# Two small loads issued by ScalarE's queue in place of SyncE's, and seven rounds of warming products in place of nine

## The chip, the cores and the metric

The kernel runs on one core of a Trainium2 chip. The metric is the device time of one execution in microseconds, as the median of several runs; lower is better. Engines are named as in the profile: PE is TensorE, DVE is VectorE, ACT is ScalarE, POOL is GpSimd, SP is SyncE. SPq and ACTq are the queues of SP and of ScalarE from which transfers are issued.

## The reference

Attention over 4 batches, 8 heads, 768 positions and 64 values a head, in which each row sees a few global positions and a local band before it, with a bias that grows with the distance; its output goes through a feed-forward layer of 512 to 2048 to 512 with a leaky activation whose slopes `alpha` are an input.

```python
scores = scale * np.matmul(q, k.transpose(0, 1, 3, 2))
keep = is_global | is_local            # from n_global = 8 and n_local = 96
scores = np.where(keep, scores - slopes * dist, -1e9)
a = softmax(scores)
x = np.matmul(a, v)                    # laid out as (3072, 512)
h = x @ w_in
g = np.maximum(h, 0.0) + alpha * np.minimum(h, 0.0)
return (g @ w_out).astype(np.float32)
```

`n_global` and `n_local` are two integers of 64 bits; they and `alpha` (2048 numbers) are the two small loads of the change. All else of the input is large.

## The kernel before

The 3072 tokens are cut into twelve units of 256. For each unit the kernel computes attention for eight heads, two at a time, then transposes the result and multiplies it with the two weight matrices, in 16 slices of 128 columns. The weights are loaded as float32 and split into two float16 parts each. Units 0 and 1 are prepared in a plain way in float32, so that work can begin before the weights are there.

The order on every engine is written out. `fast` (line 379) enters each step into a `Plan` (line 150) with a key, an engine and a cost; `Plan.order` (line 189) plays these through with costs and lags (180 after POOL, 220 after ACT, 150 after DVE, 1100 after SP, and for SP 525 an issue and 1125 before a transfer moves), and `Plan.emit` (line 293) writes the instructions in the order of the planned starts. Each engine then works through its own instructions strictly in that order.

The steps that matter here:

- `body` (line 1499) begins with the identity, the tile `ones` (line 1505), and the load of the integers into `ni` (line 1508). VectorE casts these to `nf` (line 1517).
- `warm` (line 1326) enters `WARM` products of `ones` with itself as the first step of TensorE, at the planned cost `WARM * 200`. Nothing reads their result. Each float32 product appears as two records in the trace.
- `build_bias` (line 449): POOL writes the column numbers, ScalarE makes `part` (line 484) and then the constants `ends` (line 486), VectorE builds the masks `D` from `nf` and `part` (lines 471 to 481), and eight products, `D` times a slope each, go to ScalarE or VectorE (lines 400 and 401).
- `load_first` (line 663): for unit 0, SP loads queries and keys of two heads at a time (line 677), then the values (lines 672 and 683). Behind the last of the value loads, for head 6, the same step calls `load_alpha`, defined in line 1541. `ak` (line 687) on VectorE is alpha's first reader.
- `score_pair` (line 824) enters the first scores (line 725), preceded at some places by `keep_busy` products (line 705). VectorE adds the bias and takes the smallest of the negated scores of each row (line 865), ScalarE takes the exponentials (line 875 for unit 0, line 879 for unit 1), TensorE transposes (line 908), ScalarE or VectorE copies (lines 914 and 915), TensorE multiplies with the values (line 954).
- `v_load` (line 508) and `v_sums` (line 514): the sums over the values of batch 0, from the first loads, from `firstv` and from `rawv` (line 529), from which a scale for float16 is made through a product on TensorE (`vrow`, line 555). The transposes `xp` (line 1122) and their copies `xt` (line 400) need that scale.

```python
def warm(key):
    x = buf("av", "warm", [P, 512])
    def products():
        for n in range(WARM):
            nc.tensor.matmul(x.t[:, :P], lhsT=cn["ones"], rhs=cn["ones"], start=True, stop=True)
    op("PE", key, WARM * 200, products, w=[x])
...
def values():
    nc.sync.dma_start(out=x.t[:, nk:n], in_=a["first0"][h // 2, :, nk:])
    if h == 6:
        cn["load_alpha"]()
```

Of the kernel before, what the change touches and what calls it, by code (L numbers as in the profile page):

```python
# [17 lines left out]
I32 = mybir.dt.int32  # L18
# [323 lines left out]
WLEAD = 12  # L342
VS = 6
VL = 5
WARM = 9
XPOOL, SPOOL = 0, (0, 1, 2, 3, 4, 5, 6, 7)
V0LATER, ENDS = 1, 20
F1, F1S, W0, W0S = -65, 0.5, -59, 2
# [30 lines left out]
def fast(tc, cn, a, finish):  # L379
# [3 lines left out]
    with ctx:  # L383
# [8 lines left out]
        def op(eng, key, cost, fn, r=(), w=()):  # L392
            plan.op(key, r, w, (eng, cost, fn))
# [932 lines left out]
        def warm(key):  # L1326
# [3 lines left out]
# [6 lines that stand above are left out]
# [163 lines left out]
def body(tc, a):  # L1499
    nc = tc.nc  # L1500
    with tc.tile_pool(name="const", bufs=1) as cp:
        ident = cp.tile([P, P], F32, name="ident")
        make_identity(nc, ident)
        ones = cp.tile([P, P], F32, name="ones")
        nc.vector.memset(ones, 1.0)
        alpha = cp.tile([P, NF], F32, name="alpha")
        ni = cp.tile([P, 4], I32, name="ni")
        nc.sync.dma_start(out=ni, in_=a["n"].bitcast(I32))
        nf = cp.tile([P, 4], F32, name="nf")
        n2 = cp.tile([P, 2], F32, name="n2")  # L1510
        tt = cp.tile([P, 2], F32, name="tt")
        mx = cp.tile([P, 8], F32, name="mx")
        ck = cp.tile([P, 12], F32, name="ck")
        flag = cp.tile([P, 1], I32, name="flag")
        v = nc.vector

        v.tensor_copy(out=nf, in_=ni)
        low, high = (nf.rearrange("p (n t) -> p n t", t=2)[:, :, t] for t in range(2))

        def check(line):  # L1520
            v.scalar_tensor_tensor(out=tt[:, 0:2], in0=low, scalar=0.0, in1=high, op0=ALU.is_lt, op1=ALU.add)
            v.scalar_tensor_tensor(out=n2, in0=tt[:, 0:2], scalar=4294967296.0, in1=low, op0=ALU.mult, op1=ALU.add)
            v.tensor_copy(out=mx[0:1, 4:8], in_=line)
            for j, (x, lo, hi) in enumerate((
                (n2[0:1, 0:1], 0.0, float(GL)), (n2[0:1, 1:2], 1.0, float(LOC + 1)),
                (mx[0:1, 4:5], -3.0e38, 1.0), (mx[0:1, 5:6], *RI), (mx[0:1, 6:7], *RO), (mx[0:1, 7:8], -1.0, -1.0),
            )):
                v.tensor_scalar(out=ck[0:1, 2 * j : 2 * j + 1], in0=x, scalar1=lo, scalar2=None, op0=ALU.is_ge)
                v.tensor_scalar(out=ck[0:1, 2 * j + 1 : 2 * j + 2], in0=x, scalar1=hi, scalar2=None, op0=ALU.is_le)
            v.tensor_reduce(out=tt[0:1, 0:1], in_=ck[0:1, :], axis=AX.X, op=ALU.min)  # L1530
            v.tensor_scalar(out=flag[0:1, :], in0=tt[0:1, 0:1], scalar1=1.0, scalar2=None, op0=ALU.is_lt)

        path = []

        def choose():
            path.append(nc.values_load(flag[0:1, 0:1], min_val=0, max_val=1))
            tc.mark_branch_hint_location("general", hint=path[0], engines=[
                mybir.EngineType.PE, mybir.EngineType.DVE, mybir.EngineType.Activation, mybir.EngineType.SP])

        cn = dict(ident=ident, ones=ones, alpha=alpha, ngf=n2[:, 0:1], nlf=n2[:, 1:2], check=check, choose=choose, maxima=mx, nf=nf,  # L1540
                  load_alpha=lambda: nc.sync.dma_start(out=alpha, in_=a["alpha"]))
        def finish(last):
            with tc.If(path[0] > 0, label="general") as chosen:
                general(tc, cn, a)
            with chosen.Else():
                last()

        fast(tc, cn, a, finish)
# [14 lines left out]
```

## Time and profile before

| | |
|---|---|
| median of 3 runs | 582.86 us |
| lowest, highest | 582.19, 583.93 us |
| profiled execution | 582.48 us |
| its span, first to last instruction | 580.7 us |
| TensorE busy | 567.9 us (98%) |
| VectorE busy | 487.7 us (84%) |
| ScalarE busy | 427.4 us (74%) |
| GpSimd busy | 81.0 us (14%) |
| mean granted clock of TensorE | 0.997 of full speed |

The page gives shares over the whole span. The change touches the first ten microseconds, so the tables by stretch and the timeline of the start are what to read; there each row is a group of instructions of one line with its start, its length, and in brackets how long its engine sat idle before it and what ended that.

### The profile page before, as it was taken

The page shows a single profiled execution, that of the slowest core. Times are in us where ns is not written, and L with a number is a line of the kernel's source. Part 1 is how long each engine was busy: PE and PEld are TensorE (multiplying, and loading weights), DVE is VectorE, ACT ScalarE, POOL GpSimd, SP SyncE. Part 2 cuts the span into 40 slices and gives each one's busy share as a digit, 9 for nine tenths or more (in the row PEclk, how much of TensorE's full clock was granted, in tenths as well). Part 3 has the DMA queues.
Part 4 walks back from the last instruction along what each step waited for, and adds up shares of the span by engine and source line. Part 5 has one row for each costly group of instructions (what it writes and reads, how often), then busy time and mean ns, then how long its engine had stood idle before and what let it go on. Part 6 is the DMA issues. An engine that isn't in the chain of part 4 may idle for free. (4 is left out here: it accounts for less than half of the span.)

```text
span 580.7 us, 20234 instructions
## 1 busy us (share of the span) xinstructions
PE 567.9 (98%) x8133; PEld 405.9 (70%) x8133; DVE 487.7 (84%) x1438; ACT 427.4 (74%) x1129; POOL 81.0 (14%) x194
## 2 busy tenths in 40 slices
PE   8789999999999999999999999999999999999997
PEld 7666666676666676777776777777767777767785
DVE  7899999998898898889889789789889878675443
ACT  8799999988789878776777778677578668553322
POOL 2002334223333232000001000001000000000000
PEclk9899999999999999999999999999999999999999
DMA  8997597338575279329887854528863872210001
GB/s 278 408 375 223 168 218 196 68 71 184 112 118 126 49 174 272 90 65 241 197 175 149 185 156 115 142 53 225 203 176 82 175 175 36 69 26 1 37 5 41
DMA packets 93830, 85.04 MB, mean 146 GB/s; under 512 B 71968, under 2 KB 72736, under 8 KB 93728
## 3 DMA queue, kind: packets, MB, share of 16 engines
q1 hardware_dynamic: 93584, 83.54, 57.5%
q8 instruction: 65, 1.06, 0.8%
q14 instruction: 37, 0.30, 0.2%
q10 hardware_dynamic: 144, 0.13, 0.1%
HBM read 56.65 MB, written 6.29 MB: 108 GB/s over the span
## 5 line engine op out<-in xcount | busy, mean ns | idle before, releaser
L1296 PE MATMUL o<-whl,gh 128*128 128x512 f16 (+1 forms) x800 | 230.3, 371 | 0.0
L1296 PE MATMUL o<-whl,gl 128*128 128x512 f16 (+1 forms) x400 | 148.2, 371 | 0.5 <-POOL gl L426 0.5
L1296 PEld LDWEIGHTS <-gh 128*128 128x128 f16 x800 | 71.6, 98 | 50.9
L1234 PEld LDWEIGHTS <-sw 128*128 128x128 f16 x1536 | 92.3, 98 | 14.3 <-issue 0.9
L1146 PE MATMUL h<-xt,whl 128*128 128x256 f16 x768 | 91.7, 273 | 0.9 <-DVE xt L427 0.7
L1146 PEld LDWEIGHTS <-whl 128*128 128x128 f16 x768 | 74.3, 98 | 18.6 <-issue 1.2
L879 ACT ACTIVATE pr<-pr,sm 128x192 f32<-128x192 f32 (+1 forms) x176 | 77.2, 441 | 4.0 <-DVE sm L865 3.8
L1234 PEld LDWEIGHTS <-whl 128*128 128x128 f16 x1152 | 69.6, 98 | 12.9 <-issue 0.2
L1296 PEld LDWEIGHTS <-gl 128*128 128x128 f16 x400 | 39.1, 98 | 44.8 <-POOL gl L426 1.0
L426 POOL TENSOR_TENSOR gl<-g,gh 128x256 f16<-128x256 f32 x58 | 48.8, 843 | 104.9 <-ACT gh L1161 69.0
L400 ACT ACTIVATE gh<-ga 128x512 f16<-128x512 f32 x32 | 20.2, 630 | 58.6 <-DVE ga L1273 58.6
L865 DVE CUSTOM_DVE_ANT_0 pr<-sp,D 128x192 f32<-128x192 f32 (+1 forms) x192 | 56.6, 339 | 3.7 <-PE sp L725 3.1
L1234 PE MATMUL ha<-xt,sw 128*128 128x128 f16 x768 | 53.3, 219 | 0.3 <-ACT p L1241 0.3
L1234 PE MATMUL hc<-xt,sw 128*128 128x128 f16 x768 | 53.3, 219 | 0.2 <-DVE ga L1245 0.2
L1234 PE MATMUL ha<-xt,whl 128*128 128x128 f16 x768 | 53.5, 219 | 0.0
L1004 ACT ACTIVATE ps<-pr,sm 128x192 f16<-128x192 f32 (+1 forms) x120 | 45.1, 439 | 9.7 <-DVE sm L896 4.9
L1008 DVE SCALAR_TENSOR_TENSOR ps<-pr,sm,ps 128x192 f16<-128x192 f32 (+1 forms) x128 | 47.9, 416 | 2.3 <-ACT ps L1004 2.0
L893 POOL TENSOR_SCALAR sm<-sm 128x4 f32<-128x4 f32 (+1 forms) x42 | 10.7, 254 | 245.3 <-ACT pr L879 244.7
L427 DVE SCALAR_TENSOR_TENSOR gl<-ga,gh 128x512 f16<-128x512 f32 x32 | 22.0, 689 | 13.9 <-ACT gh L400 13.8
L879 ACT ACTIVATION_READ_ACCUMULATOR pr<-pr,sm 128x1 f32 x176 | 33.5, 190 | 0.0
L427 DVE SCALAR_TENSOR_TENSOR x<-raw,x 128x672 f16<-128x672 f32 (+1 forms) x40 | 33.3, 835 | 0.1
L400 ACT ACTIVATE x<-raw 128x672 f16<-128x672 f32 (+1 forms) x33 | 24.1, 731 | 12.6 <-PE sp L725 12.4
(172 smaller groups left out, 964.9 us busy)
## 6 DMA issues: line engine op xcount, KB each, us to landing
w<-in_w_dram SPq DMA_DIRECT2D x32, 512.0 KB, 7.4
again<-in_w_dram SPq DMA_DIRECT2D x32, 512.0 KB, 5.1
raw<-in_qk_dram SPq DMA_DIRECT2D x28, 336.0 KB, 3.4
out_dram<-os SPq DMA_DIRECT2D x23, 256.0 KB, 2.9
rawv<-in_own_dram SPq DMA_DIRECT2D x10, 512.0 KB, 4.7
raw<-in_qk_dram SPq DMA_DIRECT2D x12, 272.0 KB, 3.0
gp<-v SPq DMA_DIRECT2D x48, 64.0 KB, 2.0
first<-in_qk_dram SPq DMA_DIRECT2D x4, 336.0 KB, 5.4
```

Source lines behind the costliest of these rows:

```text
L400: lambda: nc.scalar.mul(out=out(), in_=src(), mul=by.t if tile_ else by)),
L426: return e.tensor_tensor(out=out(), in0=src(), in1=hi(), op=ALU.subtract)
L427: return e.scalar_tensor_tensor(out=out(), in0=src(), scalar=val(), in1=hi(), op0=ALU.mult, op1=ALU.subtract)
L865: op("DVE", key, c_dve(n) + 10, lambda t=t, m=m, n=n, dc=dc: v.tensor_tensor_reduce(out=taken(t, m), in0=three(sp.t[:, 192 * t : 192 * t + ...
L879: op("ACT", key + 1, c_act(n, ptr=1) + 93, lambda t=t, m=m: nc.scalar.activation(out=taken(t, m), in_=taken(t, m), func=AF.Exp, bias=sm.t[ ...
L893: op("POOL", key + soon, c_pool(2 * G), lambda: nc.gpsimd.tensor_scalar(out=sm.t[:, 4 * G : 6 * G], in0=sm.t[:, 2 * G : 4 * G], scalar1=1e ...
L1004: ("ACT", c_act(n, ptr=1), lambda hi=hi, src=src, by=by: nc.scalar.mul(out=hi(), in_=src(), mul=by())),
L1008: ("DVE", Two(c_dve(n, False, 1)), lambda hi=hi, lo=lo, src=src, by=by: v.scalar_tensor_tensor(out=lo(), in0=src(), scalar=by(), in1=hi(), ...
L1146: nc.tensor.matmul(hp.t, lhsT=w.t[:, wi, wc], rhs=x.t[:, NC * xi + c, :], start=n == 0, stop=n == 3 * NC - 1)
L1234: nc.tensor.matmul(out, lhsT=weight(name, f, wi, c), rhs=x.t[:, 8 * piece + m * xi + 2 * j + c, :], start=start and p == n == 0, stop=n == ...
L1296: nc.tensor.matmul(o.t[:, cols], lhsT=g_()[:, tok], rhs=w.t[:, wi, 512 + cols.start : 512 + cols.stop], start=f == 0 and n == 0, stop=f == ...
```

## The change

The load of the integers (`ni`) and that of the slopes (`alpha`) are issued by ScalarE's queue and no longer by SyncE's. Their places in the code are the same: `ni` at the head of `body`, `alpha` behind the last of unit 0's value loads. The warming step has seven products and not nine, and its planned cost is 1400 and not 1800.

```diff
-WARM = 9
+WARM = 7
...
-        nc.sync.dma_start(out=ni, in_=a["n"].bitcast(I32))
+        nc.scalar.dma_start(out=ni, in_=a["n"].bitcast(I32))
...
-                  load_alpha=lambda: nc.sync.dma_start(out=alpha, in_=a["alpha"]))
+                  load_alpha=lambda: nc.scalar.dma_start(out=alpha, in_=a["alpha"]))
```

## Rows read from the trace of the kernel before

**Rows 1.** The page's engine shares: busy us, share of the span, instructions.
```profile
PE 567.9 (98%) x8133; PEld 405.9 (70%) x8133; DVE 487.7 (84%) x1438; ACT 427.4 (74%) x1129; POOL 81.0 (14%) x194
```
**Rows 2.** Stretches: us, busy PE, PEld, DVE, ACT, POOL; granted clock; DMA share; GB/s.
```profile
3.00:4.00 1.00, 1.00 (x7) 1.00 (x7) 0.95 (x3) 0.92 (x1) 0.00 (x0) 1.00 1.01 370
...
23.00:24.00 1.00, 0.58 (x4) 0.41 (x3) 0.93 (x8) 1.00 (x3) 0.00 (x0) 0.50 1.00 406
...
30.00:32.00 2.00, 2.00 (x68) 1.69 (x69) 2.00 (x8) 2.00 (x10) 0.10 (x1) 1.00 1.01 391
...
300.00:400.00 100.00, 100.00 (x1611) 71.80 (x1610) 86.82 (x263) 74.03 (x209) 6.16 (x22) 1.00 0.57 139
```
**Rows 3.** Timeline 0 to 9 us: start, length, engine, line, tiles; idle before and releaser.
```profile
0.73 1.28 ACT L484 ACT_TABLE_LOAD   x1 [0.73 <-PEq L1553]
0.73 0.39 SPq L1508 DMA_DIRECT2D ni<-in_n_dram  x1
...
1.05 4.21 PE L1332 MATMUL warm<-ones 128*128 128x128 f32 x18 [1.05 <-DVE ones L1505]
1.18 1.84 SPq L677 DMA_DIRECT2D first<-in_first_dram  x4
...
2.13 0.42 ACT L484 ACTIVATE part<-rel 128x256 f32<-128x256 f32 x1
...
2.40 0.35 DVE L1517 CAST nf<-ni 128x4 f32<-128x4 int32 x1 [1.41 <-DMA ni<-in_n_dram]
...
2.86 0.83 DVE L474 SCALAR_TENSOR_TENSOR D<-rel,nf,part 64x192 f32<-64x192 f32 x2
...
4.90 1.91 ACT L400 ACTIVATE D<-D 128x320 bf16<-128x320 f32 x5 [0.98 <-DVE D L481]
...
5.19 1.62 PE L725 MATMUL sp<-first 64*64 64x128 f32 x32
...
6.42 0.43 SPq L1541 DMA_DIRECT2D alpha<-in_alpha_dram  x1
...
6.77 2.24 ACT L875 ACTIVATE pr<-pr,sm 128x128 f32<-128x128 f32 x6
...
7.39 1.13 PE L705 MATMUL sp<-ident 128*128 128x128 f32 x8 [0.58 <-DVE sm L865]
```
**Rows 4.** Timeline 10 to 22 us, one engine at a time: alpha's reader, and four waits.
```profile
10.68 0.17 DVE L687 TENSOR_SCALAR ak<-alpha 128x16 f32<-128x16 f32 x1
...
16.50 0.69 DVE L529 TENSOR_REDUCE vm<-firstv 128x1 f32<-128x512 f32 x1 [1.04 <-DMA firstv<-in_first1v_dram]
...
17.49 0.46 ACT L879 ACTIVATE pr<-pr,sm 128x192 f32<-128x192 f32 x1 [1.47 <-DVE sm L865]
...
18.60 0.69 DVE L529 TENSOR_REDUCE vm<-rawv 128x1 f32<-128x512 f32 x1 [0.28 <-DMA rawv<-in_own_dram]
...
21.35 0.35 PE L555 MATMUL vrow<-vdg,ones 128*128 128x128 f32 x1 [2.41 <-DVE vdg L549]
```
**Rows 5.** DMA issues: queue, count, KB each, us to landing; last, ScalarE's issue (timeline).
```profile
first<-in_first_dram SPq DMA_DIRECT2D x1, 272.0 KB, 2.9
ni<-in_n_dram SPq DMA_DIRECT2D x1, 2.0 KB, 1.6
alpha<-in_alpha_dram SPq DMA_DIRECT2D x1, 8.0 KB, 4.2
rawv<-in_own_dram SPq DMA_DIRECT2D x1, 512.0 KB, 8.1
out_dram<-os ACTq DMA_DIRECT2D x1, 128.0 KB, 2.0
...
577.21 0.38 ACTq L1313 DMA_DIRECT2D out_dram<-os  x1
```
**Rows 6.** Timeline of ScalarE at 25 us: start, length, line, tiles; idle before and releaser.
```profile
25.39 0.69 ACT L400 ACTIVATE xt<-xp,vs 128x512 f16<-128x512 f32 x1 [0.86 <-PE xp L1122]
```

## The prediction

> **What bounds the kernel now.** I read the page's engine shares first, then a table of stretches, then the timeline of the first 24 us, and last the DMA landings. TensorE is busy 98% of the span [rows 1]. The table says where that is not so: from 300 to 400 us TensorE is busy 100.00 of 100.00 us, while from 30 to 32 us VectorE and ScalarE are both at 2.00 of 2.00 [rows 2]. So the body is bound by TensorE, and the first 50 us by VectorE and ScalarE, which run without a stop from about 20 us on. What happens earlier therefore counts only by how much it moves the time at which these two get going. No instruction of the body is changed, so what is gained or lost at the start arrives unchanged at the end, or is swallowed on the way.
>
> Before 20 us there are three chains.
> (a) The transfers. The share of the DMA engines is 1.01 from 3 to 4 us and stays near or above 1 up to 40 us [rows 2]. VectorE, at 16.50, has sat 1.04 us idle for `firstv`, and at 18.60 another 0.28 us for `rawv`; ScalarE sat 1.47 us before 17.49 [rows 4]. `rawv` leads to the row of maxima, for which TensorE sits idle 2.41 us up to 21.35 [rows 4]. So at 16 to 19 us the transfers end last, and every computing engine has spare time.
> (b) The bias chain on VectorE and ScalarE: `ni` lands, is cast at 2.40, the masks end in five products `D` on ScalarE from 4.90, and the exponentials follow from 6.77 without a gap [rows 3].
> (c) TensorE: 18 records of warming from 1.05 for 4.21 us, then the first scores at 5.19 [rows 3]. Their data, issued at 1.18, landed 2.9 us later, at 4.1 [rows 3, 5]: the scores waited for the warming, not for the data.
>
> **SP loses the load of `ni`.** SP issues `ni` at 0.73 (0.39 us) and starts on the four first loads at 1.18 [rows 3]. With `ni` gone, these start at 0.73: 0.45 us earlier, and with them the whole queue of transfers, which is issued in order and from 3 us on limited by the engines. Bytes stay the same, so I take the full 0.45 us for `firstv` and `rawv`. The lower bound is 0, if the two issues at 0.73 hold each other up, which no row shows. The upper bound adds alpha's 0.43 us of issue [rows 3], 0.88 in all; I take nothing of that, as at a DMA share of 1.0 an issue that comes sooner only queues longer: `rawv` took 8.1 us from issue to landing against 2.9 for the first load [rows 5].
>
> The Trainium skill (DMA: Bandwidth & Descriptors, "Rules for kernel authors") says that spreading loads over several issuing engines gives no bandwidth, since all use the same 16 DMA engines, and saves the sequencer's issue time only. The DMA share of 1.01 in [rows 2] agrees; by that rule the gain is the 0.45 us and not more.
>
> **ScalarE gets `ni`.** Its first work is the table load at 0.73 (1.28 us) [rows 3]. If the issue stands ahead of that, as its place in the code has it, it costs ScalarE about the 0.38 us of its one issue in this trace [rows 5]. `ni` then lands between 2.33 (1.6 us after issue, as on SP) and 2.73 (2.0 us, as ScalarE's store) [rows 5], 0 to 0.4 us later than now. The table load ends 0.38 later, so `part` at 2.13 also comes about 0.38 later; VectorE's first use of it, at 2.86, starts some 0.3 us after `part` is ready at 2.55 [rows 3], so 0.1 us of delay is left. `ends`, next on ScalarE, moves into the 0.98 us of idle time before 4.90 [rows 3]. The bias chain is 0.1 to 0.4 us late; I take 0.1, since the first row for `ni` itself is the 1.6.
>
> **ScalarE gets `alpha`.** Its issue sits in the emission after the last of the value loads. The planner gives SP 525 ns an issue, so the tenth load stands at 9 x 525 = 4725; the products `D` start there at 1500 + 180 + 325 + 220 + 1590 + 150 = 3965 (GpSimd's columns, `part`, the masks, and the lag after each) and take 381 each. The issue thus stands before or behind the third of the five `D` on ScalarE. Queued behind it are the remaining `D` and six exponentials, and for these wait the first transposes on TensorE and VectorE's next scores. Cost: 0.43 us (its issue on SP [rows 3]; 0.38 by ScalarE's store [rows 5]), and nothing if it should fall into the idle 0.98 us before 4.90 [rows 3]. I take 0.43. The reader of alpha, `ak` at 10.68 [rows 4], does not wait: issued near 5.7 and 4.2 us on the way [rows 5], alpha lands by 9.9.
>
> **Two rounds of warming less.** Four of the 18 records go, at 4.21/18 = 0.23 us about 0.9 us [rows 3]. The first scores can start near 4.3 and not 5.19; their data, at 4.1 - 0.45 = 3.65, are there. But the exponentials stand behind five `D` on ScalarE, which start when the bias chain allows: ScalarE runs from 4.90 into the exponentials at 6.77 without a break [rows 3]. The 0.9 us becomes idle time of TensorE and VectorE; I cost it at 0. Its bound on the good side is also small, since at 16.5 us the transfers come last anyway. The planner's cost of the step falls from 1800 to 1400, but it lets the scores start only after their load, at 1125 + 1148 + 1100 = 3373, so the order written out for the engines should be the same.
>
> **The sum.** Chain (b) is late by 0.1 + 0.43 = 0.53 us (bounds 0.0 and 0.83). Its cover: VectorE would have been at the `rawv` reduction 1.04 + 0.28 = 1.32 us before 18.60, at 17.28. Late by 0.53 it is there at 17.81, and `rawv` now allows 18.60 - 0.45 = 18.15. The gain stays whole up to a delay of 1.32 - 0.45 = 0.87 us, and the change turns into a loss beyond 1.32 us. So -0.45 us from 18.6 us on, carried to the end. The profiled execution is 582.48 us (span 580.7 and 1.78 around it): 582.03. The median shown is 582.86, 0.38 higher; the middle of the four executions known (582.19, 582.48, 582.86, 583.93) is 582.67, and 582.67 - 0.45 = **582.2 us**. What a measurement of this kernel can tell from no change is about 0.3%, 1.75 us; the forecast lies well inside.
>
> **Rivals.**
> *Clock, slower.* The 18 warming products took 4.21 us where eight of the same shape and type at 7.39 took 1.13 [rows 3]: 0.23 against 0.14 us each. So the warming ran at the lower level (1.2 GHz) and the later ones at 2.4 GHz, although the table prints no lower clock there. Before the rise TensorE had been in work without a break since 1.05. With the change there is 0.9 us less of that, and a longer pause before 7.39. The Trainium skill (TensorE: Matmul & The Clock Gate, "Part 1: The HAM clock gate") has the slow level as the default, which activity releases; by that rule less early work can put the rise off. Price: after the idle stretch before 21.35 the clock fell to 0.50 at 23 to 24 us [rows 2], and ScalarE waited 0.86 us for transposes made in it [rows 6]. Three such stretches, from 6 to 16 us, would be 2.6 us, and up to 3.9 if VectorE's waits add half. With chain (b)'s 0.53 that is 3.1 to 4.4 against a cover of 1.32: +1.8 to +3.1, **584.5 to 585.8**. It decides from two such stretches on (1.7 + 0.53 = 2.25, +0.9, 583.6); one is covered (0.86 + 0.53 = 1.39, +0.1). Against it: the scores follow the warming directly and the fills at 7.39 were made to go on.
> *ScalarE late.* If the table load is put ahead of the issue of `ni`, `ni` goes out at 0.73 + 1.28 = 2.01 and the bias chain is 1.28 late, with alpha 1.71: 0.39 beyond the cover, **583.1**. For it: the table load is ScalarE's first record. Against: it carries line 484, behind the place of the load.
> *No gain.* The issues at 0.73 hold each other up, or some later wait that both kernels share swallows 0.45 us: **582.7**.
> *More gain.* SP, freed of alpha too, runs 0.88 us ahead, and chain (b) is less late than 0.44: **581.8**.
>
> **How the numbers follow.** Forecast 0.45; no gain 0.18; ScalarE late 0.17; more gain 0.11; clock 0.09. The range reaches from the lowest execution with the larger gain, 582.19 - 0.88 = 581.3, rounded out to 581.1, to the lower end of the clock case, 584.5, rounded to 584.4, which also covers the highest execution, 583.93, with 0.4 on top. Over 0.3% slower means above 584.6: most of the clock case, 0.08. Over 0.3% faster means under 581.1: nothing above gives that; I leave 0.05 for a clock that falls for a shorter time around 23 us.
>
> **What the profile after would show.** The step on SP is right if the first load is issued at 0.7 to 0.8 and the wait for `rawv` ends at about 18.1. The step on ScalarE is right if the cast of `ni` starts between 2.4 and 2.8, `D` at about 5.0, and the exponentials at about 7.3. The warming is right if its record counts 14, the scores start near 4.3, and VectorE's idle time before 9.4 grows. The prediction is wrong if the cast comes at 3.5 or later (table load first), if the granted clock is low for long stretches between 6 and 20 us, if VectorE reaches the `rawv` reduction after its data, or if the time is kept at 19 us and lost later.

## The result, and the profile after

The changed kernel takes 587.31 us in the median of 8 runs (584.41 to 590.35), the kernel before 582.70 in the same comparison. The ratio is 1.0075, with a 95% interval of 1.0056 to 1.0094: slower by about 4.4 us. Two further comparisons of the same two kernels, below, gave 1.0052 [1.0032, 1.0073] and 1.0055 [1.0034, 1.0075], so 3 to 4.4 us is the size. The forecast was 582.2, with a range up to 584.4; the sign and the size were wrong. The ratios are those of the comparisons and not the quotients of the medians, which here would be 1.0079.

The profiled execution is the slowest of the eight: 590.35 us, span 588.6. Its timeline of the first 12 us, to be read against [rows 3] (start, length, engine, line, operation and tiles; in brackets the idle time before and what ended it):

```profile
0.73 0.41 ACTq L1508 DMA_DIRECT2D ni<-in_n_dram  x1
0.73 1.82 SPq L677 DMA_DIRECT2D first<-in_first_dram  x4
1.05 3.36 PE L1332 MATMUL warm<-ones 128*128 128x128 f32 x14 [1.05 <-DVE ones L1505]
1.17 1.28 ACT L484 ACT_TABLE_LOAD   x1 [1.17 <-PEq L1553]
...
2.79 1.47 ACT L486 ACTIVATE ends<-ones 128x1536 f16<-128x1536 f32 x1
...
3.77 0.17 DVE L1517 CAST nf<-ni 128x4 f32<-128x4 int32 x1 [2.77 <-DMA ni<-in_n_dram]
...
4.34 2.27 PE L725 MATMUL sp<-first 64*64 64x128 f32 x32
...
9.30 0.33 ACTq L1541 DMA_DIRECT2D alpha<-in_alpha_dram  x1
...
9.74 1.91 ACT L400 ACTIVATE D<-D 128x320 bf16<-128x320 f32 x5 [5.48 <-DMA first<-in_first_dram]
10.24 0.29 DVE L865 CUSTOM_DVE_ANT_0 pr<-sp,D 128x128 f32<-128x128 f32 x1 [3.59 <-ACT D L400]
...
11.20 2.04 PE L705 MATMUL sp<-ident 128*128 128x128 f32 x8 [4.60 <-DVE sm L865]
```

ScalarE has done `ends` at 4.26. The next instruction of its order is the issue of alpha, and that goes out at 9.30. The five `D`, whose input VectorE had ready near 6, start at 9.74 and not at 4.90. The releaser named there is the landing of a load `first`: no data that `D` needs, but what the issue ahead of `D` waited for. VectorE then waits 3.59 us for `D`, and TensorE 4.60 us for VectorE.

The stretches of the changed kernel (columns as in [rows 2]):

```profile
7.00:8.00 1.00, 0.00 (x0) 0.00 (x0) 0.00 (x0) 0.00 (x0) 0.00 (x0) 1.00 1.06 226
...
10.00:11.00 1.00, 0.00 (x0) 0.00 (x0) 0.76 (x6) 1.00 (x4) 0.00 (x0) 0.50 0.97 367
...
12.00:13.00 1.00, 1.00 (x6) 0.95 (x5) 0.52 (x6) 1.00 (x4) 0.22 (x3) 0.50 1.13 321
```

From 7 to 8 us no computing engine does anything. After that pause TensorE's granted clock is 0.50, the lower of its two levels (1.2 GHz), and it is still there at 12 to 13 us. The eight fills take 2.04 us where they took 1.13 [rows 3].

The two waits that the prediction's cover was made of, in the changed kernel (timeline; compare [rows 4]):

```profile
23.35 0.68 DVE L529 TENSOR_REDUCE vm<-rawv 128x1 f32<-128x512 f32 x1
...
26.10 0.46 PE L555 MATMUL vrow<-vdg,ones 128*128 128x128 f32 x2 [1.70 <-DVE vdg L549]
```

VectorE no longer waits for `rawv`: it comes 4.75 us later than before, long after the data, and `vrow` is 4.75 us late as well (26.10 against 21.35).

**What the issue waits for.** The list of instructions in the built program names it. Every load takes one of eight semaphores in turn, and its issue waits until the load that had that semaphore before has landed. In the changed kernel:

```
ACT 4  L486  ACTIVATE ends<-ones 128x1536 [waits DVE_49]
ACT 5  L1541 DMA alpha<-in_alpha_dram 128x16 [waits DMAHW7_49]
ACT 6  L400  ACTIVATE D_236<-D 128x320 [waits DVE_49,Pool_49]
...
SP  7  L672  DMA first_2_179<-in_first_dram 128x260
SP  8  L672  DMA first_4_181<-in_first_dram 128x260 [waits DMAHW0_49]
SP  9  L683  DMA far_220<-in_far_dram 64x520 [waits DMAHW1_49]
```

`ni`, the four first loads and the next three have semaphores 0 to 7 fresh; the eighth load, that of the values of heads 2 and 3, has semaphore 7. Alpha is the sixteenth load in the order of the program, so its turn is semaphore 7 again. The eighth load was issued at 3.70 and landed 5.6 us later (the DMA view of the changed kernel: queue, operation, count, size, us from issue to landing):

```profile
first<-in_first_dram SPq DMA_DIRECT2D x1, 130.0 KB, 5.6
```

3.70 + 5.6 = 9.30, the start of alpha's issue, as near as a view in tenths can tell (the trace has the last event of that semaphore at 9.28). In the kernel before, the same kind of wait stood on SP, where nothing but other loads is queued behind it. SP's table of waits for 0 to 30 us of the kernel before (total, times, longest) shows it:

```profile
SPq L604 <- DMA w<-in_w_dram: 5.6, 6, 1.6
...
SPq L691 <- DMA first<-in_first_dram: 0.7, 2, 0.3
SPq L669 <- DMA first<-in_first_dram: 0.5, 2, 0.3
```

What these waits cost on SP no run shows; only loads stood behind them. Alpha itself did not wait there: as the twelfth load it took over semaphore 3, whose load had landed at 6.07 by the trace's events, and SP, busy with other issues until then, sent it out at 6.42 [rows 3]. I did not read that view before predicting.

The Trainium skill (DMA: Bandwidth & Descriptors, "Anatomy of one DMA — SWDGE (gpsimd) path") says that DMA engines do not wait on semaphores, and that any such wait takes place on the issuing sequencer, before dispatch. That section follows a transfer issued by GpSimd; the 5.48 us of ScalarE's idle time, ahead of one issued by ScalarE, agree.

Apart from buffer numbers and the number of warming products, TensorE, VectorE and GpSimd have the same instructions in the same order in both kernels; SP and ScalarE differ by the two loads alone. So the planner's changed cost for the warming moved nothing, as forecast.

### The profile page after: what moved, and what is told of

It is laid out like the page before. It is cut to its first block, busy times and chain, and to the rows that moved or that the text cites. A ratio compares the mean times of both kernels' runs of the same rounds, so it can differ in the third digit from the quotient of the medians.

```text
span 588.6 us, 20226 instructions
## 1 busy us (share of the span) xinstructions
PE 571.3 (97%) x8129; PEld 408.1 (69%) x8129; DVE 487.4 (83%) x1438; ACT 427.5 (73%) x1129; POOL 82.3 (14%) x194
## 5 line engine op out<-in xcount | busy, mean ns | idle before, releaser
L426 POOL TENSOR_TENSOR gl<-g,gh 128x256 f16<-128x256 f32 x58 | 50.1, 866 | 104.5 <-ACT gh L1161 68.1
L427 DVE SCALAR_TENSOR_TENSOR gl<-gb,gh 128x512 f16<-128x512 f32 x32 | 22.0, 688 | 14.3 <-ACT gh L400 14.3
```

What stands on the lines that cost most here:

```text
L426: return e.tensor_tensor(out=out(), in0=src(), in1=hi(), op=ALU.subtract)
L427: return e.scalar_tensor_tensor(out=out(), in0=src(), scalar=val(), in1=hi(), op0=ALU.mult, op1=ALU.subtract)
```

## The experiments

All ratios are against the kernel before on the same chip, with a 95% interval.

| kernel | median us | before us | ratio |
|---|---|---|---|
| `ni` on ScalarE only | 581.96 | 582.14 | 0.9997 [0.9974, 1.0020] |
| alpha on ScalarE only | 585.11 | 582.14 | 1.0053 [1.0027, 1.0079] |
| seven rounds only | 583.81 | 582.14 | 1.0009 [0.9983, 1.0036] |
| both loads, nine rounds | 586.01 | 582.14 | 1.0054 [1.0029, 1.0079] |
| the change again | 585.12 | 581.91 | 1.0052 [1.0032, 1.0073] |
| the change, alpha issued right behind `ni` | 582.47 | 581.91 | 1.0006 [0.9984, 1.0029] |
| alpha alone, at the head of ScalarE | 582.26 | 581.91 | 1.0007 [0.9990, 1.0023] |
| the change, 24 rounds | 583.97 | 581.91 | 1.0034 [1.0017, 1.0051] |
| alpha on ScalarE, issued earlier | 587.03 | 582.58 | 1.0064 [1.0039, 1.0088] |
| `ni` on ScalarE, a second load of it on SP (one run) | 580.95 | 582.58 | - |
| the change, third time | 586.38 | 582.58 | 1.0055 [1.0034, 1.0075] |
| the change, 24 rounds, again | 585.03 | 582.58 | 1.0051 [1.0026, 1.0076] |

Seven of the times came out beyond the range expected for them (quoted below), by 0.03 to 0.6 us; five of these came out low, in comparisons whose kernel before also stood lower than the first one's 582.70. Only for seven rounds does the miss come near a rival.

And where the profiled execution of each stood, in us from its start (timelines): ScalarE's first `D`, the first transposes on TensorE (line 908), VectorE's reduction of `rawv`, the row of maxima on TensorE, and the first product with the output weights (line 1296).

| kernel | alpha issued on ScalarE | `D` | transposes | `rawv` | `vrow` | line 1296 |
|---|---|---|---|---|---|---|
| before | - | 4.90 | 9.16 | 18.60 | 21.35 | 36.98 |
| the change | 9.30 | 9.74 | 14.45 | 23.35 | 26.10 | 41.41 |
| the change again | 9.29 | 9.73 | 14.44 | 22.96 | 25.71 | 40.09 |
| the change, third time | 7.61 | 8.05 | 12.76 | 21.80 | 24.55 | 39.87 |
| `ni` only | - | 6.18 | 9.41 | 17.98 | 20.74 | 35.12 |
| alpha only | 8.38 | 8.87 | 13.47 | 21.40 | 24.15 | 38.53 |
| seven rounds only | - | 4.90 | 8.47 | 19.37 | 22.12 | 37.37 |
| both, nine rounds | 9.12 | 9.57 | 14.28 | 22.71 | 25.46 | 39.84 |
| alpha right behind `ni` | 1.17 | 6.13 | 9.35 | 17.92 | 20.67 | 36.08 |
| alpha alone at the head | 0.73 | 4.96 | 9.36 | 18.67 | 21.43 | 37.22 |
| alpha earlier | 7.76 | 9.58 | 14.27 | 23.09 | 25.84 | 41.16 |
| `ni` twice | - | 5.01 | 8.55 | 18.53 | 21.29 | 36.54 |
| the change, 24 rounds | 9.13 | 9.57 | 12.80 | 21.71 | 26.89 | 41.27 |
| the change, 24 rounds, again | 9.00 | 9.45 | 12.67 | 22.57 | 27.71 | 43.68 |

### One part at a time

`ni` alone:

```diff
-        nc.sync.dma_start(out=ni, in_=a["n"].bitcast(I32))
+        nc.scalar.dma_start(out=ni, in_=a["n"].bitcast(I32))
```

> Only the integers on ScalarE's queue; slopes on SP, nine rounds. Theory S (the issue of alpha on ScalarE waits for the semaphore of a value load and holds ScalarE up): alpha is not there, so no more than a few tenths: ni lands near 3.7, D starts near 6.2 in place of 4.90, which is 1.3 us late against a cover of 1.32 us; 582.3 to 583.5. Rival N (the late landing of ni is what costs): 585 or more. Rival W (the two missing rounds and the clock): no change, 582.7.

No change in the time: 0.9997. Its timeline:

```profile
3.86 0.17 DVE L1517 CAST nf<-ni 128x4 f32<-128x4 int32 x1 [2.87 <-DMA ni<-in_n_dram]
...
6.18 1.91 ACT L400 ACTIVATE D<-D 128x320 bf16<-128x320 f32 x5 [1.92 <-DVE D L481]
...
17.98 0.69 DVE L529 TENSOR_REDUCE vm<-rawv 128x1 f32<-128x512 f32 x1 [0.46 <-DMA rawv<-in_own_dram]
...
20.74 0.46 PE L555 MATMUL vrow<-vdg,ones 128*128 128x128 f32 x2 [1.78 <-DVE vdg L549]
```

`ni` is cast 1.46 us later than before and `D` starts 1.28 us later, and still VectorE waits for `rawv`, which is 0.62 us earlier. By the transposes, 1.28 us have shrunk to 0.25 (table). So rival N falls, and the part of the forecast that gave SP 0.45 us is seen in this profile; in the time it can't be told from nothing.

Alpha alone:

```diff
-                  load_alpha=lambda: nc.sync.dma_start(out=alpha, in_=a["alpha"]))
+                  load_alpha=lambda: nc.scalar.dma_start(out=alpha, in_=a["alpha"]))
```

> Only the slopes on ScalarE's queue; integers on SP, nine rounds. Theory S: the issue of alpha waits for the transfer whose semaphore it takes over, here that of the first load of far values, which landed at 8.4 us before; ScalarE is idle from about 4 to 8.5 us, D starts near 8.9 and the row of maxima on TensorE is 3 to 4.5 us late; 585.5 to 587.5. Rivals N and W: no change beyond ScalarE's 0.43 us, 582.7 to 583.1.

This part alone makes the kernel slower, by 1.0053. The place in the turn is another, since `ni` and the first loads are on one queue again: semaphore 6, the far values. Timeline of ScalarE, then the DMA view of that load, issued at 3.54:

```profile
8.38 0.38 ACTq L1541 DMA_DIRECT2D alpha<-in_alpha_dram  x1
8.87 1.55 ACT L400 ACTIVATE D<-D 128x320 bf16<-128x320 f32 x4 [4.95 <-DMA far<-in_far_dram]
```

```profile
far<-in_far_dram SPq DMA_DIRECT2D x1, 130.0 KB, 4.8
```

3.54 + 4.8 = 8.34, and the issue goes out at 8.38. The earlier user changed, and the wait followed it.

Seven rounds alone (`WARM = 7`):

> Only the warming cut from nine to seven rounds. Theory S and rival N: no change, 582.2 to 583.2, scores start at 4.3 and wait. Rival W: the clock rises later or falls between 6 and 16 us, 584 or more.

1.0009: no change that can be told, though the interval still allows a loss of 2.1 us and a gain of 1.0. The scores start at 4.34, `D` at 4.90 as before, the transposes at 8.47, and the granted clock is 1.00 in every stretch from 6 to 22 us. But the medians stand 1.67 us apart, more than the ratio says, and 583.81 is only 0.2 under rival W's 584. So the profile does not show W's mechanism, but the time alone does not refute W, and the shorter warming may cost some tenths or more. What decides stands below: the loss is there with nine rounds, and it is gone with seven when alpha's issue does not wait.

The change without its last line, so both loads with nine rounds:

> Both loads on ScalarE's queue, nine rounds of warming: the change without its last line. Theory S: as slow as the change, 586.5 to 588. Rival W: most of the loss is gone, under 584.5. Rival N: as slow as the change, but then also when only ni is moved.

1.0054: the loss is there with nine rounds too. The clock falls in this kernel as in the change (stretches, columns as above):

```profile
9.00:10.00 1.00, 0.00 (x0) 0.00 (x0) 0.00 (x0) 0.43 (x2) 0.00 (x0) 0.50 1.03 379
12.00:13.00 1.00, 1.00 (x6) 0.78 (x4) 0.34 (x4) 1.00 (x5) 0.10 (x2) 0.50 1.07 387
```

So the low clock follows ScalarE's wait, not the shorter warming.

### The same issue without a wait

The change itself, for comparison on this chip:

> The change as it stands, on the same chip as the next three. All theories: 585.5 to 588.

1.0052. Then the same with alpha issued right behind `ni`, where the semaphores are fresh:

```diff
-                  load_alpha=lambda: nc.scalar.dma_start(out=alpha, in_=a["alpha"]))
+                  load_alpha=lambda: None)
...
         nc.scalar.dma_start(out=ni, in_=a["n"].bitcast(I32))
+        nc.scalar.dma_start(out=alpha, in_=a["alpha"])
```

> The change, with alpha issued right behind ni at the head of ScalarE's queue, where no semaphore has an earlier user. Theory S: the loss is gone, 581.5 to 583; ScalarE's D starts near 6.3 (ni still late), no idle time of 5 us. Rival: that any issue of alpha on ScalarE, or ni late and fewer rounds together, costs the 4 us: 585 or more.

1.0006: the loss is gone, with both loads on ScalarE and seven rounds kept. ScalarE now issues both in its first microsecond and starts `D` at 6.13, when VectorE has it ready:

```profile
6.13 0.47 ACT L400 ACTIVATE D<-D 128x320 bf16<-128x320 f32 x1 [1.38 <-DVE D L481]
```

Alpha alone at the head of ScalarE, `ni` on SP, nine rounds:

> Integers on SP, nine rounds, alpha alone at the head of ScalarE's queue. Theory S: no loss, 581.7 to 582.9, D near 5.0 and ni landing 0 to 0.5 us later beside alpha's packets. Rival: 585 or more as with alpha in its old place on ScalarE.

1.0007, `D` at 4.96. An issue of alpha on ScalarE costs nothing that can be told here (the intervals leave room for 1.7 and 1.3 us), as long as it waits for nothing.

### The issue put earlier

This tests whether it was the late place of the issue, among loads under way, that made it wait:

```diff
-                    if h == 6:
+                    if h == 0:
                         cn["load_alpha"]()
```

(on the kernel with alpha alone on ScalarE)

> Slopes on ScalarE's queue, issued with the first of the value loads and not the last: on ScalarE the issue then stands ahead of the constants `ends` and takes over the semaphore of the load of the values of heads 0 and 1. Theory S: it waits for that landing, near 7.9 us; ScalarE is idle from 2.6 to 7.9, then does `ends` (1.47 us) and starts D near 9.8; 585 to 587. Rival (the wait comes from the issue standing late, among loads already under way): an earlier place cures it, 583 or less.

1.0064, no better. The semaphore is number 5, that of the values of heads 0 and 1, issued at 3.07 and landed 4.7 us later, at 7.77. The DMA view, and ScalarE's timeline:

```profile
first<-in_first_dram SPq DMA_DIRECT2D x1, 130.0 KB, 4.7
```

```profile
7.76 0.38 ACTq L1541 DMA_DIRECT2D alpha<-in_alpha_dram  x1
8.19 1.48 ACT L486 ACTIVATE ends<-ones 128x1536 f16<-128x1536 f32 x1 [5.64 <-DMA first<-in_first_dram]
```

Third earlier user, third landing, third match. The other two profiles in which alpha waits for semaphore 7 agree: with both loads and nine rounds the load lands at 3.70 + 5.4 = 9.10 and the issue goes out at 9.12, in the third profile of the change at 3.70 + 3.9 = 7.60 and 7.61. `ends`, which stood ahead of the wait before, now stands behind it and adds its 1.48 us. The expectation of 7.9 and of `D` near 9.8 came out as 7.76 and 9.58.

### Why `ni` was late

A second load of the integers, into a tile that nothing reads, put ahead of SP's first large load, with `ni` on ScalarE:

```diff
+        ni2 = cp.tile([P, 4], I32, name="ni2")
-        nc.sync.dma_start(out=ni, in_=a["n"].bitcast(I32))
+        nc.scalar.dma_start(out=ni, in_=a["n"].bitcast(I32))
+        nc.sync.dma_start(out=ni2, in_=a["n"].bitcast(I32))
```

> Integers on ScalarE's queue, with a second load of the same integers, into a tile that nothing reads, ahead of the first large loads on SP; alpha on SP, nine rounds. Theory C (the packets of ni took turns with those of the first large load): the large loads start 0.45 us later again, ni lands about 1.6 us after its issue and the cast starts near 2.4 to 2.6. Rival Q (ScalarE's queue is itself slower): ni lands 3.0 us after its issue and the cast starts near 3.8. Time 581.5 to 583.5 by both.

One run, 580.95 us, so only its profile is read. From issue to landing (DMA view at 0.73 us: this kernel's two loads first, then that of the kernel with `ni` alone moved):

```profile
ni<-in_n_dram SPq DMA_DIRECT2D x1, 2.0 KB, 1.8
ni<-in_n_dram ACTq DMA_DIRECT2D x1, 2.0 KB, 1.9
```

```profile
first<-in_first_dram SPq DMA_DIRECT2D x1, 272.0 KB, 2.9
ni<-in_n_dram ACTq DMA_DIRECT2D x1, 2.0 KB, 3.1
```

ScalarE's queue brings the integers in 1.9 us when the large load starts later, and in 3.1 beside it. Rival Q falls. The packets of the trace say how: before, the 128 packets of `ni`, 16 bytes each, moved between 1.75 and 2.03 us, ahead of the first large packet at 2.22; in the change they moved between 1.96 and 3.21, among packets of 2176 bytes that had begun at 1.74.

The Trainium skill (DMA: Bandwidth & Descriptors, "Queues, rings and completion order") has each DMA engine serve the queues in turn, packet by packet. The spread of `ni` over 1.25 us agrees. It is a rule that spoke against this change, and the prediction did not weigh it.

### What the low clock adds

The change with 24 rounds of warming, their planned cost kept, so that TensorE is in work while ScalarE waits:

```diff
-                for n in range(WARM):
+                for n in range(24):
...
-            op("PE", key, WARM * 200, products, w=[x])
+            op("PE", key, 1400, products, w=[x])
```

> The change with 24 rounds of warming, so that TensorE is in work through most of ScalarE's wait (about 1.05 to 9 us) and its clock has no reason to fall; its planned cost stays that of seven rounds. Theory S with the clock as a follower: ScalarE still waits until 9 us, the low stretch at 9 to 16 us is gone, 583.5 to 585.5. Theory S without the clock: 586 to 588 unchanged. Rival W (it is the clock alone): 583 or less.

1.0034 against the change's 1.0052 on the same chip. Repeated with more rounds, beside the change for a third time:

> The change as it stands, on the same chip as the next, for what the clock adds. 585 to 587.

> The change with 24 rounds of warming again, with more rounds. If the low clock after ScalarE's wait adds about 1 us: 1.0 to 1.3 us below the change on this chip, and the loss against the kernel before 2 us. If it adds nothing: within 0.4 us of the change.

1.0051 against 1.0055. The medians stand 1.15 and 1.35 us under the change's, but by the ratios it is 1.0 and 0.2 us, and the intervals overlap in both comparisons: whether the longer warming saves anything is not shown. The profiles tell why it is hard to see. Stretches of the first of the two runs:

```profile
9.00:10.00 1.00, 1.00 (x32) 0.72 (x24) 0.00 (x0) 0.43 (x2) 0.00 (x0) 1.00 1.07 280
12.00:13.00 1.00, 1.00 (x20) 0.63 (x19) 0.36 (x5) 1.00 (x5) 0.10 (x2) 1.00 1.09 415
18.00:19.00 1.00, 0.00 (x0) 0.00 (x0) 0.37 (x2) 0.17 (x1) 0.00 (x0) 1.00 1.03 410
22.00:23.00 1.00, 1.00 (x29) 0.88 (x23) 1.00 (x3) 1.00 (x6) 0.00 (x0) 0.50 1.07 414
```

The clock is high at 9 to 13 us. From `D` to the transposes it takes 4.71 us in all three profiles of the change and in the one with nine rounds, and 3.23 here (table). So 1.5 us of the delay at that point go with the low clock. But TensorE then sits idle again up to 19.00, and the clock is at 0.50 at 22 to 23 us, which takes the gain back in this execution: `vrow` stands at 26.89. The second run with 24 rounds is alike, with `vrow` at 27.71. The idle time has no releaser in the profile (timelines of the two):

```profile
19.00 0.27 PE L954 MATMUL av<-far,pt 64*64 64x65 f32 x2 [1.59 <-issue]
```

```profile
19.76 0.37 PE L954 MATMUL av<-far,pt 64*64 64x65 f32 x2 [2.32 <-issue]
```

What held TensorE up in the middle of a step whose operands were there is open. It is the same product in both, and the DMA packets hold one hint: a packet of 16 KB, of the kind that the DMA view calls `instruction`, moved from 16.64 to 17.74 us in the first profile and from 17.22 to 18.32 in the second, and the pauses ended 1.3 and 1.4 us after it. TensorE may have waited for its own instructions, of which the longer warming puts 68 more ahead (34 products and 34 weight loads by the records); that is argued and not shown. Either way the kernel with 24 rounds is not the change with the low clock taken away and nothing else.

In the third profile of the change, alpha's issue went out at 7.61 and not at 9.30, since the load ahead of it landed earlier:

```profile
7.61 0.33 ACTq L1541 DMA_DIRECT2D alpha<-in_alpha_dram  x1
8.05 0.47 ACT L400 ACTIVATE D<-D 128x320 bf16<-128x320 f32 x1 [3.79 <-DMA first<-in_first_dram]
...
24.55 0.35 PE L555 MATMUL vrow<-vdg,ones 128*128 128x128 f32 x1 [1.71 <-DVE vdg L549]
```

`D` comes 1.68 us sooner than in the second profile (9.73), and `vrow` 1.16 us sooner (25.71).

No kernel of these beat the kernel before by more than the intervals allow.

## Why the prediction was wrong

**The step that failed** is "ScalarE gets `alpha`", with its price of 0.43 us and the bounds 0 to 0.43. I counted the issue's own time and named what is queued behind it, but not what the issue itself waits for. It waited 5 us for the landing of an unrelated load. The term measured 4.84 us at `D` (9.74 against 4.90), eleven times the price; alpha alone, which waited for another load, made it 3.97 (8.87). The place was misread as well: I had the issue at the third of the five `D`, and it stands ahead of all five. The bounds came from the lengths of issue rows, on SP and on ScalarE; neither shows a wait, because a wait stands ahead of an issue and not in its length. The row for it was in the table of SP's waits.

With that term right, the sum would have had the sign and nearly the size. By its own arithmetic VectorE reaches the `rawv` reduction at 17.28 + 4.84 = 22.12 us. The first two profiles of the change have 23.35 and 22.96, 1.2 and 0.8 later. The low clock's 1.5 us at the transposes, less cover, would account for that; this is argued from the sizes and not shown. Against 18.60 that is a loss of 4.4 to 4.75 us at this point, 4.75 at `vrow` in the first profile and 4.36 in the second.

**"ScalarE gets `ni`"**: the bound of 0.4 us was too narrow. `ni` was cast 1.37 us late, because a small load on its own queue shares the DMA engines with the large load issued at the same moment. I took the rows of 1.6 and 2.0 us as bounds, but in neither did another load start beside the small one. It cost nothing that can be told in the end: the kernel with `ni` alone is at 0.9997. Here the cover was larger than computed. I moved chain (b) as a rigid piece, and did not count a wait within it (timeline of the kernel before):

```profile
6.43 0.29 DVE L865 CUSTOM_DVE_ANT_0 pr<-sp,D 128x128 f32<-128x128 f32 x1 [0.97 <-PE sp L725]
```

VectorE sat idle 0.97 us for the first scores, so `D` can be late by that much before VectorE's part is. 1.28 - 0.97 = 0.31, and 0.25 is what was left at the transposes.

**"SP loses the load of `ni`"**: right in its mechanism, and near in its size. The first load goes out at 0.73, and with `ni` alone `rawv` is ready 0.62 us and `vrow` 0.61 us earlier, against the forecast 0.45. The four profiles in which SP's first large load goes out at 1.18 and VectorE waits for `rawv` have its reduction at 18.53 to 19.37, the two in which it goes out at 0.73 at 17.92 and 17.98: earlier in both, but the spread is larger than the term. In the change it is worth nothing, since VectorE arrives after its data.

**"Two rounds of warming less"**: priced at 0; measured 1.0009 [0.9983, 1.0036], which allows 0 and does not prove it.

**The rivals.** "ScalarE late" had the right engine and the wrong cause: the table load stands behind the issue of `ni` (1.17 after 0.73), and the delay came from alpha. "Clock, slower" came true in what it described, a clock at 0.50 from 9.74 to 16.6 us and a loss in its direction, but as a follower of ScalarE's wait: with nine rounds it falls as well, and with seven alone the profile shows no stretch under 1.00 between 6 and 22 us. Its size, 1.8 to 3.1 us, was for a cause that did not act.

**What the profile after was to show**: that VectorE would reach the `rawv` reduction after its data was on the list of signs that the prediction is wrong, and it is what happened. Two more signs on it came: the low clock between 6 and 20 us, and a cast after 3.5 (3.77), though not from the table load that the list names for it. The warming's signs came as forecast: 14 records, scores from 4.34. A wait of ScalarE for another load was not on the list.

The profiled execution lost 3 us more later on. TensorE waited 1.56 and 0.47 us at 281 us for transposes that a DMA brings (`pt`), after which the clock was low for 3.4 us. It shows in the first and third profiles of the change and not in the second, so it is part of the spread of 584.41 to 590.35. Why these transposes were late is not settled.

## What to carry to other kernels

Before a load is moved to the queue of a computing engine, ask what its issue waits for, not only how long it takes: where loads share a few semaphores in turn, the issue waits for an earlier load to land, and everything behind it on that engine waits along. On a queue of loads alone the same wait holds up only loads and is easily overlooked, so look for it there, in the table of that queue's waits, before moving. A load that must go on a computing engine belongs at the head, ahead of the first re-use of a semaphore: here that took the loss from 1.0052 to 1.0006.

## What the runs showed of the hardware

- A load of 2 KB issued at the same moment as one of 272 KB on another queue landed after 3.0 to 3.1 us, and after 1.9 us when the large one came 0.45 us later. A queue of its own gives a small load no right of way.
- An issue that waits on a semaphore holds its whole engine: 3.79 to 5.64 us of idle time on ScalarE in the five profiles read for it, in each of which the issue went out within 0.05 us of the landing of the load in question.
- In a pause of 4.6 us in TensorE's work, which another engine caused, its clock fell to 0.50 and stayed there for 6.8 us in the change, so that a delay of 4.8 us at `D` was 5.3 us at the transposes, although the chain has slack between the two. From `D` to the transposes it took 4.7 us with the clock low and 3.2 with it high.
